# A decode-step kernel: second MLP layer on four column groups, folded output rows, early loads on two queues

## The chip, the cores and the metric

The kernel runs on one core of a Trainium2 chip. The metric is the device time of one execution in microseconds (us), lower is better. "Landing" is the moment at which a transfer's last bytes have arrived; "granted clock" is the share of TensorE's full clock that the profile shows in a stretch.

## The reference, cut to what matters

One decode step of a transformer block with modulation, for 8 batches: attention with grouped queries over a cache of 8192 positions, then an MLP with squared ReLU.

```python
mod = (_silu(c) @ w_mod).reshape(8, 6, 1, -1)          # sa, ca, ga, sb, cb, gb
h = _layernorm(x) * (1 + ca) + sa
x = x + ga * attention(h, k_cache, v_cache, wq, wo)     # caches: [8, 8, 8192, 128] bf16
h = _layernorm(x) * (1 + cb) + sb
r = relu(h @ w1 + b1); y = (r * r) @ w2 + b2            # w1: [512, 1792], w2: [1792, 512]
x = x + gb * y                                          # [8, 1, 512] bf16
```

The two caches are 268 MB; all other inputs together are about 15 MB.

## The kernel before

The caches come in 64 units of 4 MB (two heads of one batch each) into a ring of four slots. The MLP weights take over a slot at the very end, in six transfers. Every load but two of 8 KB (c and x) goes through SyncE's queue:

```python
# load n of the 64; d_w1/d_w2 come after the last of them
dep = [released.get(s), d_wo if n == NSLOT else None]
loaded[n] = dma("sync", s_ring[s], lambda e: e.dma_start(slot(s), src), dep)
...
load(0); load(1)            # ahead of A_wo in the queue
dma(... b1 ...); d_bb = dma(... b2 ...)
d_wo = dma("sync", s_wo, ...)
load(2); load(3)
...
d_w2 = [dma("sync", s_w2[i], ...) for i, (a, z, j) in
        enumerate(((0, 4, 4), (4, 8, 4), (8, 12, 4), (12, 14, 2)))]
```

The end of the program, with cuts. The activations are kept transposed (features on partitions), so the second layer uses the weights as the stationary operand and 8 batch columns as the moving one, and the result must be transposed back:

```python
for k in range(KT):                       # first layer: 4 x 14 matmuls, all f for each k
    if k == KT - 1: ...                   # variance, square root, reciprocal behind 42 of 56
    for f in range(FT): ...
for f in range(FT):                       # second layer
    for k in range(KT):
        matmul(yT_ps[:, k, :], W2v[:, f, k * 128:(k + 1) * 128], hidT[:, f, :],
               deps=[k_sq[f // 8], d_w2[f // 4]])
for cc in range(2): ...                   # residual x1T put into o_ps by 4 matmuls with IDENT
k_y2 = tensor_tensor(y2T, yT_ps, mod(5), mult)                 # 128x32
for cc in (1, 0):
    ... 2 matmuls: o_ps[64 * cc: 64 * cc + B] += y2T^T         # transposes back
    ... copy to out_sb: VectorE for one half, ScalarE for the other
    d_o.append(dma(("sync", "scalar")[cc], ...))               # 8 rows of 512 bytes each
Pg.wait("sync", d_o)
```

## Time and profile before

| | before |
|---|---|
| time, median of 3 | 668.38 us |
| span of the profiled execution | 666.7 us |
| bytes read | 283.66 MB |
| last landing of second-layer weights (landing records of the trace) | 663.33 us |
| output transfers issued | 664.85 and 664.92 us |
| last landing of the output | 666.27 us |

The page is read from its DMA rows: the transfers fill the span. The end is read from the timeline and from the landing records. The lines are shown in the prediction below.

### The profile page before, as it was taken

The page shows a single profiled execution, that of the slowest core. Times are in us where ns is not written, and L with a number is a line of the kernel's source. Part 1 is how long each engine was busy: PE and PEld are TensorE (multiplying, and loading weights), DVE is VectorE, ACT ScalarE, POOL GpSimd, SP SyncE. Part 2 cuts the span into 40 slices and gives each one's busy share as a digit, 9 for nine tenths or more (in the row PEclk, how much of TensorE's full clock was granted, in tenths as well). Part 3 has the DMA queues.
Part 4 walks back from the last instruction along what each step waited for, and adds up shares of the span by engine and source line. Part 5 has one row for each costly group of instructions (what it writes and reads, how often), then busy time and mean ns, then how long its engine had stood idle before and what let it go on. Part 6 is the DMA issues. An engine that isn't in the chain of part 4 may idle for free.

```text
span 666.7 us, 15924 instructions
## 1 busy us (share of the span) xinstructions
PE 528.3 (79%) x7259; PEld 352.2 (53%) x7259; DVE 307.9 (46%) x587; ACT 264.3 (40%) x307; POOL 20.5 (3%) x79
## 2 busy tenths in 40 slices
PE   3494976898849987599858988499776998589887
PEld 2383732675328742477316753287424773277535
DVE  1262741466316652367415662167513673146633
ACT  2151631466115651166314661166512663146611
POOL 7400000000000000000000000000000000000000
PEclk9696998799969999699998999799997999879996
DMA  9999999999999999999999999999999999999997
GB/s 375 437 406 441 419 433 433 425 434 431 438 427 433 433 434 427 434 434 425 434 431 438 427 431 434 434 427 431 438 425 434 433 436 427 431 434 434 427 420 285
DMA packets 12189, 283.85 MB, mean 426 GB/s; under 512 B 1261, under 2 KB 1297, under 8 KB 3601
## 3 DMA queue, kind: packets, MB, share of 16 engines
q1 hardware_dynamic: 12128, 283.65, 99.3%
q8 instruction: 9, 0.15, 0.1%
q10 hardware_dynamic: 48, 0.02, 0.0%
q14 instruction: 4, 0.02, 0.0%
HBM read 283.66 MB, written 0.01 MB: 425 GB/s over the span
## 4 chain that ended last, share of the span: by engine, by line
PE 52%; DMA 38%; ACT 6%; DVE 2%; issue 1%; SPq 0%; DVEq 0%
PE PS L488 36%; DMA ring<-in_A_k_cache_dram 33%; PE PS L505 9%; ACT P_sb L582 5%; DMA ring<-in_A_v_cache_dram 4%; DMA ring<-in_A_wq_dram 2%; PE PS L636 2%; PE PS L478 1%; ACT KTb L493 1%; DVE O_sb L656 1%; PE PS L472 1%; PE PS L594 1%; DVE Pm L608 0%; PE PS L614 0%; PE PS L773 0%
## 5 line engine op out<-in xcount | busy, mean ns | idle before, releaser
L488 PE MATMUL PS<-IDENT,ring 128*128 128x128 bf16 x4096 | 267.1, 227 | 56.2 <-DMA ring<-in_A_k_cache_dram 56.2
L488 PEld LDWEIGHTS PS<-IDENT,ring 128*128 128x128 bf16 x4096 | 246.5, 102 | 104.8 <-DMA ring<-in_A_k_cache_dram 57.4
L493 ACT ACTIVATE KTb<-PS 128x1024 bf16<-128x1024 bf16 x192 | 196.5, 1024 | 236.6 <-PE PS L488 236.6
L495 DVE COPY KTb<-PS 128x1024 bf16<-128x1024 bf16 x320 | 210.0, 688 | 146.5 <-PE PS L488 144.4
L636 PE MATMUL PS<-ring,Pm 128*32 128x512 bf16 x1018 | 67.2, 409 | 24.8 <-DMA ring<-in_A_v_cache_dram 23.9
L505 PE MATMUL PS<-KTb,Qb 128*32 128x512 bf16 x1024 | 79.0, 385 | 4.5 <-ACT KTb L493 4.5
L656 DVE CAST O_sb<-PS 128x512 bf16<-128x512 f32 x31 | 21.5, 692 | 112.7 <-PE PS L636 112.7
L636 PEld LDWEIGHTS PS<-ring,Pm 128*32 128x32 bf16 x1018 | 26.5, 101 | 61.8 <-DMA ring<-in_A_v_cache_dram 33.7
L535 ACT ACTIVATE KTb<-PS 32x192 bf16<-32x192 f32 (+1 forms) x18 | 5.6, 310 | 110.0 <-PE PS L472 103.9
L582 ACT ACTIVATE P_sb<-PS,negm 128x1024 bf16<-128x1024 f32 x32 | 35.2, 1111 | 20.2 <-DVE negm L577 20.2
L478 PE MATMUL PS<-ONES 128*128 128x512 f32 x80 | 42.1, 630 | 0.0
L472 PE MATMUL PS<-IDENT 128*128 128x512 bf16 x112 | 33.4, 380 | 0.0
L594 PE MATMUL PS<-IDENT,P_sb 128*128 128x128 bf16 x256 | 19.9, 220 | 15.4 <-ACT P_sb L582 15.4
L608 DVE COPY Pm<-PS 64x512 bf16<-64x512 bf16 x48 | 20.2, 421 | 25.0 <-PE PS L594 24.5
L594 PEld LDWEIGHTS PS<-IDENT,P_sb 128*128 128x128 bf16 x256 | 14.4, 98 | 25.1 <-ACT P_sb L582 25.1
L505 PEld LDWEIGHTS PS<-KTb,Qb 128*32 128x32 bf16 x1024 | 15.4, 94 | 21.0 <-ACT KTb L493 8.5
L512 DVE TENSOR_REDUCE m<-PS 128x1 f32<-128x512 f32 x32 | 22.1, 689 | 6.6 <-PE PS L505 6.6
L660 PEld LDWEIGHTS PS<-SEL,O_sb 128*128 128x128 bf16 x124 | 5.8, 97 | 30.0 <-DVE O_sb L656 30.0
L478 PEld LDWEIGHTS PS<-ONES 128*128 128x128 f32 x80 | 12.7, 190 | 10.6 <-issue 10.6
L660 PE MATMUL PS<-SEL,O_sb 128*128 128x8 bf16 x124 | 7.8, 169 | 12.3 <-DVE O_sb L656 12.0
L472 PEld LDWEIGHTS PS<-IDENT 128*128 128x128 bf16 x112 | 9.9, 104 | 10.1 <-issue 7.2
L543 PE MATMUL PS<-wo_sb,KTb 128*32 128x512 bf16 x192 | 11.8, 380 | 3.3 <-ACT KTb L535 3.3
(134 smaller groups left out, 147.0 us busy)
## 6 DMA issues: line engine op xcount, KB each, us to landing
ring<-in_A_k_cache_dram SPq DMA_DIRECT2D x32, 4096.0 KB, 34.0
ring<-in_A_v_cache_dram SPq DMA_DIRECT2D x31, 4096.0 KB, 27.8
ring<-in_A_wq_dram SPq DMA_DIRECT2D x1, 4096.0 KB, 19.8
wo_sb<-in_A_wo_dram SPq DMA_DIRECT2D x1, 4096.0 KB, 47.3
ring<-in_w_mod_dram SPq DMA_DIRECT2D x1, 3072.0 KB, 10.5
ring<-in_A_v_cache_dram SPq DMA_DIRECT2D x1, 2048.0 KB, 22.5
ring<-in_B_w_dram SPq DMA_DIRECT2D x3, 512.0 KB, 19.2
ring<-in_B_w_dram SPq DMA_DIRECT2D x1, 1344.0 KB, 17.8
```

The costliest lines, as they stand in the source:

```text
L472: ts = [op("tensor", lambda e: e.matmul(bank(at).rearrange("p (a r) -> p a r", a=4), IDENT[:, :], rhs)) for _ in range(n)]
L478: ts = [op("tensor", lambda e: e.matmul(bank(at).rearrange("p (a r) -> p a r", a=4), ONES[:, :], rhs)) for _ in range(n)]
L488: t = op("tensor", lambda e, j=j, i=i: e.matmul(STG[j][:, i, :], src[:, 32 * k + 8 * j + i, :], IDENT[:, :], is_transpose=True), [loaded[n ...
L493: stg_free[j] = op("scalar", lambda e, j=j, dst=dst: e.activation(dst, STG[j], ACT.Copy), [t])
L495: stg_free[j] = op("vector", lambda e, j=j, dst=dst: e.tensor_copy(dst, STG[j]), [t])
L505: t = op("tensor", lambda e, hf=hf, q=q, rhs=rhs: e.matmul(PS[32 * q:32 * (q + 1), k, :], Qb[:, 2 * p + hf, :], rhs, start=(p == 0 and hf ...
L512: return op("vector", lambda e: e.tensor_reduce(m4[:, k:k + 1], bank(k), AX.X, ALU.max), [t])
L582: exps.append(op("scalar", lambda e, k=k: e.activation(P_sb[:, k, :, :, :], bank(k).rearrange("p (i x) -> p i x", i=8).unsqueeze(2).to_bro ...
L594: t = op("tensor", lambda e, k=k, i=i: e.matmul(STG[k][:, i, :], P_sb[:, k, i, :, :].rearrange("p h x -> p (h x)"), IDENT[:, :], is_transp ...
L608: done.append(op("vector", lambda e, dst=dst, frm=frm: e.tensor_copy(dst, frm), [t, k_pm]))
L636: t = op("tensor", lambda e, m=m, cg=cg, p=p, vt=vt, Obank=Obank: e.matmul(Obank[32 * cg:32 * (cg + 1), :], lhs[:, p, 32 * m:32 * m + 32], ...
L656: t = op("vector", lambda e, osb=osb, Obank=Obank: e.tensor_copy(osb, Obank), [t])
```

## The change

Its intent has three parts. At the **end**, batches become the rows of the second layer's output: the hidden activations (128x32, 8 columns used) become the stationary operand, the weights move, and four blocks of 128 output columns go to four column groups of TensorE (32 columns of its array each, `tile_position=(0, 32 * k)`). The result is then already in output order, so the transposes back fall away; two additions fold four groups into two rows of 512 bytes. The first layer runs half by half. At the **start**, the first two loads and the biases go to ScalarE's queue and A_wo moves ahead of them; early copies go from ScalarE to VectorE; GpSimd builds fewer selection matrices. In the **loop**, four permute copies stay on VectorE and the projection goes behind 16 value matmuls.

```diff
-            dep = [released.get(s), d_wo if n == NSLOT else None]
+            dep = [released.get(s), d_wo if n == 2 * NSLOT - 1 else None, k_wm if eng == "scalar" else None]
...
-        k_mr1 = op("scalar", lambda e: e.activation(mod_r[:, 1, :], bank(1), ACT.Copy), [t])
+        k_mr1 = op("vector", lambda e: e.tensor_copy(mod_r[:, 1, :], bank(1)), [t])
...
-        load(0)
-        load(1)
-        dma("sync", s_bb, lambda e: e.dma_start(
+        load(0, "scalar")
+        load(1, "scalar")
+        dma("scalar", s_bb, lambda e: e.dma_start(
...
-        for k in range(KT):
-            if k == KT - 1:
+        for hh, (fa, fz) in enumerate(((0, 8), (8, FT))):
+            for k in range(KT):
+                if (hh, k) == (0, 2):
...
-                    yT_ps[:, k, :], W2v[:, f, k * 128:(k + 1) * 128], hidT[:, f, :],
-                    start=False, stop=(f == FT - 1), skip_group_check=True), [k_sq[f // 8], d_w2[f // 4]])
+                    y_ps[32 * k:32 * (k + 1), :], hidw[:, f, :], W2v[:, f, 128 * BLK[k]:128 * (BLK[k] + 1)],
+                    start=False, stop=(f == FT - 1), tile_position=(0, 32 * k), skip_group_check=True),
+                    [k_sq[f // 8], d_w2[f // 4]])
+        t = op("vector", lambda e: e.tensor_tensor(y_sb, y_ps, mod5[:], ALU.mult), [t])
+        for h in range(2):
+            rows = slice(64 * h, 64 * (h + 1))
+            t2 = op("vector", lambda e, h=h, rows=rows: e.tensor_tensor(
+                out_sb[:, h, :], y_sb[rows, :], x1_sb[rows, :], ALU.add), [t, k_res])
```

## The prediction

> **What bounds the kernel now.** I read the page first, its DMA rows and queue table before its engine rows. The engine rows say that TensorE is busy 79% of the span, which looks like a TensorE kernel; the DMA rows say otherwise. The columns of the DMA and GB/s rows are 40 equal slices of 16.7 us.
>
> ```profile
> DMA  9999999999999999999999999999999999999997
> GB/s 375 437 406 441 419 433 433 425 434 431 438 427 433 433 434 427 434 434 425 434 431 438 427 431 434 434 427 431 438 425 434 433 436 427 431 434 434 427 420 285
> ...
> q1 hardware_dynamic: 12128, 283.65, 99.3%
> ```
>
> The reader is to see that the transfers never pause: 283.65 MB go through one queue, 99.3% of all time of the 16 DMA engines is spent on its packets, and only the first and the last slice carry less. Divided by about 433 GB/s the bytes alone take some 655 us of a span of 666.7. The chain of waits agrees in its own way: DMA 38% of the span, and TensorE's 52% is mostly key tiles worked off between two loads that the chain also ends on. So everything between the first microseconds and the last load counts only through the DMA stream. The chance of a change lies in how early the stream starts, how evenly it runs, and what is left to do after its last byte.
>
> Then I read the windows at the end (start:end, length, busy time of PE, weight loads, VectorE, ScalarE, GpSimd, each with its count, then granted clock, DMA share, GB/s):
>
> ```profile
> 658.00:659.00 1.00, 0.72 (x22) 0.72 (x23) 0.51 (x3) 0.00 (x0) 0.00 (x0) 0.50 1.06 424
> 659.00:660.00 1.00, 1.00 (x27) 1.00 (x26) 0.00 (x0) 0.00 (x0) 0.00 (x0) 0.50 0.98 393
> 660.00:661.00 1.00, 0.68 (x16) 0.58 (x15) 0.32 (x2) 0.27 (x1) 0.00 (x0) 0.50 1.00 393
> 661.00:662.00 1.00, 0.32 (x12) 0.32 (x13) 0.88 (x5) 0.00 (x0) 0.00 (x0) 0.50 0.67 264
> 662.00:663.00 1.00, 0.87 (x34) 0.81 (x31) 0.21 (x1) 0.00 (x0) 0.00 (x0) 0.50 0.27 92
> 663.00:664.00 1.00, 1.00 (x27) 0.70 (x24) 0.19 (x1) 0.00 (x0) 0.00 (x0) 0.50 0.00 0
> ```
>
> The DMA share is full up to 661 us and gone by 663: the stream runs on underneath the whole MLP, because the MLP weights are its last 4 MB. The view of the tensor that holds these weights gives the last landing:
>
> ```profile
> L682 SPq DMA_DIRECT2D ring<-in_B_w_dram x4: 885/1444/5533, 641.0 to 649.9; - x4
> DMA to landing us min/median/max: 13.5/18.1/19.2
> ```
>
> The last of four pieces of the second layer's weights was issued at 649.9 and took 13.5 us to land: 663.4. (The landing records in the trace give 660.2, 661.5, 662.7 and 663.35 for the four pieces.) Now the timeline of the end:
>
> ```profile
> 661.68 2.06 PE L773 MATMUL PS<-KTb,ring 128*128 128x8 bf16 x56 [1.00 <-DVE KTb L768]
> ...
> 663.78 0.19 DVE L781 TENSOR_TENSOR KTb<-PS,modT 128x32 bf16<-128x32 f32 x1 [1.56 <-PE PS L773]
> ...
> 664.03 0.38 PE L786 MATMUL PS<-IDENT,KTb 128*8 128x128 bf16 x4
> 664.44 0.37 ACT L793 ACTIVATE KTb<-PS 8x256 bf16<-8x256 f32 x1 [3.90 <-PE PS L786]
> 664.49 0.41 DVE L791 CAST KTb<-PS 8x256 bf16<-8x256 f32 x1 [0.51 <-PE PS L786]
> 664.85 0.30 ACTq L794 DMA_DIRECT2D out_dram<-KTb  x1
> 664.92 0.31 SPq L794 DMA_DIRECT2D out_dram<-KTb  x1
> ```
>
> The reader is to see two limits that meet. The 56 second-layer matmuls run without a visible pause from 661.68 to 663.74, so the row names VectorE's square as what released them. But their last 8 need the piece that lands at 663.35, and by count they begin at 663.74 - 8 x 2.06/56 = 663.45. Had TensorE been ready any earlier, it would have waited for the weights.
>
> **What the Trainium skill says.** "DMA: Bandwidth & Descriptors", section "Where 436 GB/s comes from", gives a ceiling of 435.2 GB/s for a core's 16 engines; the steady slices above show 425 to 438, so the trace agrees: there is no rate left to win. The same page, "Issuing engines are not separate DMA queues", says that transfers issued from several engines run on the same 16 engines and interleave, and that only issue time is saved. The kernel before has no two large transfers on two queues at once, so its trace cannot show this; it is my reason to give the second queue no value. "TensorEngine Tiling (Array Packing)", section "Performance Considerations", proposes swapping stationary and moving operand with column tiling where one side is narrow, which is this change. The trace has the form already: 24 matmuls of L543 (128x32 stationary, 512 moving columns, four column groups) take 1.48 us, or 0.06 each. "VectorE: DVE Perf Modes", section "Two Vector instructions with no wait between them", says that an instruction whose operand starts in another group of 32 partitions than the last one's is held until earlier ones finish; nothing before shows it, but I count the two final adds as serial for it.
>
> **The change, part by part.**
>
> Start. Loads 0 and 1 move to ScalarE's queue and wait for the modulation matmul (about 14.8 us); the output-projection weights move ahead of them. The stream is full from about 2.5 us either way, and w_mod and A_wq, 7.3 MB, still cover it to about 21 us, so no gap opens. From 15 to some 42 us two queues share the engines. A_wq may land 2 to 3 us after the 21.1 us of now, and the first key tiles (30.8 now) start up to 4 us later. That delay is absorbed: the row for unit 2 shows TensorE idle 10.39 us for its load at 61.61, and the first value slot comes free at 96.0 with a load that takes 23.8 us to land although its own bytes need 9.7, so about 14 us of transfers lie queued ahead. Worth: 0.
>
> GpSimd loses some 40 selects (20.5 us busy now), ScalarE two copies of 0.6 us. GpSimd ends at 29.4, before the first keys at 30.8. Worth: 0. The permute copies in the loop go to VectorE, four of about 0.36 us instead of two, and the projection goes behind 16 value matmuls; in the loop they lie in the idle time of the V half. In the last batch: values from the landing at 649.4 to 650.45, projection 1.48 to 651.95, its copy 0.69 to 652.7; the next value matmuls wait for weights until 652.5 anyway, as now. Worth: 0.
>
> First layer. Now the variance matmul comes behind 42 of 56 matmuls; after, behind 16. From 658.28: 16 x 0.036 = 0.58, variance 0.57, so 659.4; square root, reciprocal and their gaps 0.6 as now, 660.0; the first half's matmuls end there too. Three VectorE steps of 0.25 give the first square at about 660.8 instead of 661.63: 0.8 us earlier. But this feeds the second layer, which now waits for the pieces at 660.2, 661.5, 662.7 and 663.35. The 0.8 us disappear.
>
> Second layer. 56 matmuls of 0.037 us (bound by 128-column weight loads) become 14 rounds of four, 128 moving columns each; at the granted clock of 0.50 a round is a quarter of the 0.43 us that L402's rounds of 512 columns took at that clock, 0.107 us: 1.5 us instead of 2.06. Only the last piece counts: two rounds, 0.21, and about 0.17 from start to result beyond the streaming (the 4 matmuls of L786 took 0.38 for two columns-passes of 0.107 per group). So 663.38 + 0.38 + 0.03 = 663.8. Now it is 663.74. Worth: 0.
>
> After the second layer. Out go the multiplication 0.19, four transposing matmuls 0.38, and the copies 0.37/0.41 with their gaps: 663.78 to 664.92. In come a multiplication of 128x128 and two additions of 64x128. VectorE's rows are 192 ns at 32 columns, 202 at 48, 222 to 225 at 64: about 160 + 1 per column, so 0.29 at 128. The additions, bf16 in SBUF, I take as 0.25. With gaps of 0.035: 663.82 + 0.29 + 0.035 + 0.25 + 0.035 + 0.25 = 664.68, transfers at 664.7 to 664.75. Saved: about 0.2 us. The output transfer (1.8 us to the end) has the same eight rows of 512 bytes on two queues.
>
> Sum: about -0.2 us of 668.38. I add another -0.1 because the slowest DMA engine, which sets each landing, trails the fastest by 2.2 us, and another mix of packets can only partly even that out. Predicted 668.1.
>
> **The rivals.** (1) The compute chain, not the weights, is the end's bound: then the 0.8 of the first layer, 0.5 of the second and 0.2 behind it all come through, 1.5 us, giving 666.9. For it: the timeline names VectorE as releaser, not the DMA. Against it: the landing at 663.35. (2) Two queues change the stream itself. The 4 KB rows of the output projection run at slices of 406 instead of 433; mixing them with 32 KB rows could hide up to 0.5 us of that, giving 667.6; or fetches of program code, which the trace shows stretching single packets from 1.2 to 1.7 us, fall on the slowest engine once more: 668.7. (3) The late A_wq starves the stream in the first batch. The queue would have to lose the 14 us; I see 4. It would make 670 or more.
>
> **Range and chances.** Bounded by rival 1 plus a little on one side and one bad code fetch on the other: 667.0 to 668.9. A gain of 2% would need 13 us, while start and tail together hold about 6; a loss of 2% needs rival 3 in earnest. So within 2%: 0.985.
>
> **What would show it.** The stream full from 2.5 us to about 661; the last weights landing at 663.0 to 663.7; TensorE waiting on the DMA for B_w2 pieces, where now no such wait appears; second-layer matmuls ending within 0.45 us of the last landing; about 0.9 us from there to the output transfers. I am wrong if the last landing moves by more than 0.5 us, if any slice before the last drops below 400 GB/s, or if the second layer ends well after the landing.

## The result, and the profile after

| | before | after |
|---|---|---|
| time, median of 4 in the same rounds | 668.42 us (668.37 to 669.41) | 668.65 us (668.50 to 668.85) |
| ratio, 95% interval | | 1.000 (0.9983 to 1.0017) |
| span of the profiled execution | 666.7 | 666.9 |
| A_wq landed / first key transposes | 21.0 / 30.83 | 23.2 / 31.82 |
| last landing of second-layer weights | 663.33 | 663.48 |
| last landing of the output | 666.27 | 666.25 |

A ratio is the mean time of one kernel's runs over that of the other's of the same rounds, so it is not quite the ratio of the medians. The numbers for landings are the last of the increments that the trace records for a transfer's semaphore, in us from the span's start.

The page of the changed kernel answers to the rows of before as follows (same columns):

```profile
GB/s 376 414 429 433 428 428 435 428 430 432 432 432 432 430 432 432 428 436 428 436 427 436 430 428 432 432 432 428 436 428 436 427 436 430 430 430 432 436 414 282
...
q1 hardware_dynamic: 11824, 275.26, 96.3%
q10 hardware_dynamic: 350, 8.41, 3.0%
```

The 8.4 MB of loads 0 and 1 and the biases are now on the second queue, and 96.3% + 3.0% of the engines' time is what one queue held before. The second and third slice, 437 and 406 before, are 414 and 429: the slower 4 KB rows of A_wo are spread over another time, and nothing is won in the sum. The start came as worked out; the first key tiles, before and then after:

```profile
30.84 5.71 PE L488 MATMUL PS<-IDENT,ring 128*128 128x128 bf16 x64 [5.11 <-DMA ring<-in_A_k_cache_dram]
```

```profile
31.82 6.43 PE L483 MATMUL PS<-IDENT,ring 128*128 128x128 bf16 x64 [3.81 <-DMA ring<-in_A_k_cache_dram]
```

They wait for load 0 in both, and start one microsecond later in the second. The windows of the changed kernel at the end:

```profile
661.00:662.00 1.00, 0.84 (x33) 0.70 (x32) 0.88 (x5) 0.00 (x0) 0.00 (x0) 0.50 0.62 246
662.00:663.00 1.00, 0.29 (x16) 0.06 (x8) 0.00 (x0) 0.00 (x0) 0.00 (x0) 0.50 0.33 119
663.00:664.00 1.00, 0.92 (x24) 0.47 (x24) 0.02 (x1) 0.00 (x0) 0.00 (x0) 0.50 0.00 0
```

Between 662 and 663 TensorE was busy 0.87 before and is busy 0.29 now: it stands idle, and the view of the weights' tensor says for what:

```profile
L676 SPq DMA_DIRECT2D ring<-in_B_w_dram x4: 432/2596/4702, 640.6 to 646.4; - x4
...
  PE PS L771: 0.7, 1
  PEld PS L771: 0.2, 1
...
DMA to landing us min/median/max: 17.0/18.6/20.0
```

The last piece, issued at 646.4, took 17.1 us to land by its landing record: 663.5. (The view's minimum of 17.0 is that of the piece before it.) No such wait for weights is named in the view of before. The last piece is issued 3.5 us earlier than before (646.4 against 649.9; why is not shown) and takes 3.6 us longer to land (17.1 against 13.5), so the earlier issue wins nothing. The timeline of the end:

```profile
661.19 1.07 PE L771 MATMUL PS<-ring,hidw 128*32 128x128 bf16 x32 [0.16 <-DVE hidw L766]
...
662.97 0.95 PE L771 MATMUL PS<-ring,hidw 128*32 128x128 bf16 x24 [0.71 <-DMA ring<-in_B_w_dram]
663.52 0.14 PEld L771 LDWEIGHTS PS<-ring,hidw 128*32 128x32 bf16 x8 [0.19 <-DMA ring<-in_B_w_dram]
663.98 0.29 DVE L775 TENSOR_TENSOR KTb<-PS,mod 128x128 bf16<-128x128 f32 x1 [2.03 <-PE PS L771]
664.30 0.45 DVE L778 TENSOR_TENSOR KTb<-KTb 64x128 bf16<-64x128 bf16 x2
664.78 0.37 SPq L781 DMA_DIRECT2D out_dram<-KTb  x1
664.78 0.31 ACTq L781 DMA_DIRECT2D out_dram<-KTb  x1
```

The second layer starts 0.49 us earlier than before (661.19 against 661.68), pauses twice for weights, and ends 0.2 us later (663.92 against 663.74), behind weights that landed 0.15 us later. Multiplication and two additions then take 0.8 us where multiplication, transposes and copies took 1.1.

### The profile page after: what moved, and what is told of

Its sections match the earlier page's. It is cut to its first block, busy times and chain, and to the rows that moved or that the text cites. A ratio compares the mean times of both kernels' runs of the same rounds, so it can differ in the third digit from the quotient of the medians.

```text
span 666.9 us, 15813 instructions
## 1 busy us (share of the span) xinstructions
PE 534.7 (80%) x7247; PEld 354.5 (53%) x7247; DVE 316.2 (47%) x611; ACT 257.6 (39%) x288; POOL 13.6 (2%) x37
## 3 DMA queue, kind: packets, MB, share of 16 engines
q1 hardware_dynamic: 11824, 275.26, 96.3%
## 4 chain that ended last, share of the span: by engine, by line
PE 53%; DMA 36%; ACT 7%; DVE 2%; SPq 1%; issue 1%; ACTq 0%; DVEq 0%
PE PS L483 36%; DMA ring<-in_A_k_cache_dram 33%; PE PS L500 9%; ACT P_sb L575 5%; DMA ring<-in_B_w_dram 3%; PE PS L629 2%; PE PS L473 1%; ACT KTb L488 1%; DMA KTb<-in_A_x_dram 1%; DVE O_sb L650 1%; SPq L676 1%; PE PS L467 1%; PE PS L587 1%; PE PS L393 1%; DVE Pm L601 1%
## 5 line engine op out<-in xcount | busy, mean ns | idle before, releaser
L629 PE MATMUL PS<-ring,Pm 128*32 128x512 bf16 x1018 | 69.8, 414 | 40.7 <-DMA ring<-in_A_v_cache_dram 39.8
L467 PE MATMUL PS<-IDENT 128*128 128x512 bf16 x104 | 31.7, 380 | 0.0
L654 PEld LDWEIGHTS PS<-R,O_sb 128*128 128x128 bf16 x124 | 5.7, 96 | 28.7 <-DVE O_sb L650 28.7
L536 PE MATMUL PS<-wo_sb,KTb 128*32 128x512 bf16 x192 | 18.9, 556 | 0.0
L654 PE MATMUL PS<-R,O_sb 128*128 128x8 bf16 x124 | 7.8, 169 | 12.4 <-DVE O_sb L650 12.0
L530 DVE CAST KTb<-PS 32x192 bf16<-32x192 f32 (+1 forms) x34 | 11.8, 346 | 6.1 <-PE PS L517 5.3
```

Source lines behind the costliest of these rows:

```text
L467: ts = [op("tensor", lambda e: e.matmul(bank(at).rearrange("p (a r) -> p a r", a=4), IDENT[:, :], rhs)) for _ in range(n)]
L629: t = op("tensor", lambda e, m=m, cg=cg, p=p, vt=vt, Obank=Obank: e.matmul(Obank[32 * cg:32 * (cg + 1), :], lhs[:, p, 32 * m:32 * m + 32], ...
```

## The experiments

My theory after the two traces: the DMA stream sets the end. What lies before it costs nothing, what lies beside it is hidden, and the three tenths of a microsecond behind it are the only thing that the change can move. The rivals were a cost of the second queue that hides a larger gain at the end, and a middle bound by TensorE. Twelve kernels ran (one of them is the changed kernel unedited, and one the padded kernel again), four to a call, each call on one chip and beside the kernel before.

### The two halves of the change alone

head_only is the changed kernel with the old end put back; tail_only is the kernel before with the new end. Together they hold each part of the change once.

```diff
 # head_only, from the changed kernel
-  (first layer by halves, y_ps on column groups, fold)
+  (old first layer, yT_ps, transposes back, two copies)
 # tail_only, from the kernel before: the reverse
```

> The changed kernel with the old second layer and output put back: early loads on two queues, early copies on VectorE, shorter GpSimd start, new order in the last-batch projection. Stream theory (the end is the last weight landing plus some 3.4 us): the stream is full either way, 668.4, within 0.2 of the kernel before. Rival, two queues cost the slowest DMA engine time: 668.6 to 668.9, and the last landing of the second-layer weights comes 0.2 to 0.4 us later than the 663.33 of before.

> The kernel before with only the new second layer, first-layer order and folded output. Stream theory: the 0.14 us by which the output transfers are issued earlier in the changed kernel, so 668.2 to 668.4. Rival, the two queues ate a larger gain of the tail: 667.9 or less.

Measured: head_only 668.88 us, tail_only 668.55, the kernel before 668.62 (ratios 1.0004 and 0.9996, intervals 0.9991 to 1.0017 and 0.9984 to 1.0008). The time of head_only fits the rival, but its stated sign is missing: its last weights landed at 663.23, no later than the 663.33 of before. So the 0.26 us, which lie within the interval, are made elsewhere. tail_only missed its 668.2 to 668.4; in its trace the last weights landed 0.3 us later than before, and that scatter is larger than the gain looked for. The landing records and SyncE's last instructions, read from the raw records of all traces, show where (us from the span's start; "branch" is SyncE's jump out of the program, which comes after its wait for the output):

```
kernel        weights  output   from weights  SyncE    from output
              landed   landed   to output     branch   to branch
before        663.33   666.27   2.94          666.34   0.07
head_only     663.23   666.18   2.95          666.61   0.43
before_half   659.27   662.22   2.95          662.30   0.08
after         663.48   666.25   2.77          666.49   0.24
tail_only     663.64   666.38   2.74          666.46   0.08
after_late    663.27   666.05   2.78          666.28   0.23
after_again   663.38   666.16   2.78          666.40   0.24
after_half    658.58   661.35   2.77          661.60   0.25
after_pad     663.43   666.21   2.78          666.23   0.02
after_pad2    662.96   665.72   2.76          665.74   0.02
after_nofold  663.29   666.15   2.86          666.17   0.02
```

Three things are to be read. The column "from weights to output" has two values: 2.94 to 2.95 with the old end, 2.74 to 2.78 with the new one. The new end is worth 0.16 to 0.21 us, about 0.17, whatever else differs. The column "from output to branch" has a gap of 0.23 to 0.43 in five kernels, all with the change's start, and 0.02 to 0.08 in the others. And the weights of the nine whole kernels of the table (all but the two cut by half) land between 662.96 and 663.64 without an order that follows the start: 663.33 and 663.64 with one queue, 662.96 to 663.48 with two. The 0.15 us by which they landed later in the changed kernel's first trace lie within this scatter. An effect of the second queue smaller than it, either way, is not excluded: only two of the nine traces have one queue.

### How much the computation has in reserve

Both kernels load only the first of four pieces of the second-layer weights and use it for all (wrong result). The landing then no longer holds the second layer up.

```diff
-  for i, (a, z, j) in enumerate(((0, 4, 4), (4, 8, 4), (8, 12, 4), (12, 14, 2)))]
+  for i, (a, z, j) in enumerate(((0, 4, 4),))]
...
-  W2v[:, f, ...],      [k_sq[f // 8], d_w2[f // 4]]
+  W2v[:, f % 4, ...],  [k_sq[f // 8], d_w2[0]]
```

> The kernel before, but only the first of four pieces of the second-layer weights is loaded and used for all (wrong result on purpose); 1.31 MB less at the end of the stream, some 3.1 us of it. If in the kernel before the chain of computation and the landings meet, as the prediction had it, taking the landings away gives almost nothing: 668.2 to 668.4. If the landing alone set its end, about 667.

> The same cut in the changed kernel (wrong result on purpose). Stream theory: its computation is ready about 1.2 us before the last landing, so without it the second layer ends at about 662.7 instead of 663.94 and the time is 667.4, 1.0 to 1.4 below the changed kernel and about 0.9 below the cut kernel before. If the new chain of computation is no shorter, there is no difference: 668.4.

Measured: 667.84 us for the cut kernel before (0.9983 of the whole one, 0.9969 to 0.9998), 667.15 for the cut changed kernel (0.9973, 0.9958 to 0.9987). The first is lower than the 668.2 to 668.4 of a tie; the second is lower than its 667.4 too, and the 0.69 us between them are less than the 0.9 expected. One row of each timeline tells why for the first: the second layer, first of the cut kernel before, then of the cut changed kernel.

```profile
661.47 1.65 PE L773 MATMUL PS<-KTb,ring 128*128 128x8 bf16 x56 [0.99 <-DVE KTb L768]
```

```profile
661.08 1.69 PE L771 MATMUL PS<-ring,hidw 128*32 128x128 bf16 x56 [0.17 <-DVE hidw L766]
```

The 56 old matmuls take 1.65 us when nothing holds them up, not the 2.06 of the whole kernel's row. That row had 0.41 us of pauses for weights merged into it. The trace of the kernel before shows one of them in the weight loads of the same matmuls, which come to a stop until 0.1 us after the third piece's landing at 662.69, with no releaser named:

```profile
662.80 0.86 PEld L773 LDWEIGHTS PS<-KTb,ring 128*128 128x128 bf16 x24 [0.19 <-issue]
```

The kernel before was bound by the landing, by about 0.4 us; I had read it as a tie. (The other 0.2 us between the traces of the whole and the cut kernel is an earlier start of the second layer, 661.47 against 661.68.) And the 56 new ones take 1.69: at the granted clock of 0.50 the swap of operands buys nothing on TensorE. What the change does win in the computation is the shorter first layer and the shorter way out. With the landings gone the times show 667.84 - 667.15 = 0.69 us of it, with the landings in place 0.17. The chain itself is shorter by more: from the first layer's first matmul to the last output issue it takes 664.30 - 658.07 = 6.23 us in the first trace and 663.62 - 658.50 = 5.12 in the second, 1.1 less. The first layer began 0.43 us later in the second trace, whose piece of weights landed 0.50 later; both lie within the scatter of the stream.

### Whether the stream really sets the end

The second half of one K load in batch 3 is left out in both kernels (wrong, though an average over 8192 nearly even weights hides it from the comparison).

```diff
+  w = UNIT // 2 if n == 24 else UNIT
-  loaded[n] = dma(eng, s_ring[s], lambda e: e.dma_start(slot(s), src), dep)
+  loaded[n] = dma(eng, s_ring[s], lambda e: e.dma_start(slot(s)[:, 0:w], src[:, 0:w]), dep)
```

> The changed kernel with the second half of one K load of batch 3 left out (wrong result on purpose): 2.10 MB less in the middle of the stream, at 431.7 GB/s 4.86 us. Stream theory: all of it comes through at the end, 663.6 to 664.0. Rival, TensorE's keys or the hand-over of slots bound the middle: less than half comes through, 666 or more.

> The same cut in the kernel before: stream theory 663.4 to 663.8; rival 666 or more.

Measured: 663.62 us for the changed kernel, whose uncut twin took 668.49: 4.87 less, and 4.86 was expected. The kernel before took 663.39 and 663.42 in two runs and 664.41 and 665.23 in two others (median 663.92, against 668.36); in its profiled run, one of the two longer ones, the last piece of weights landed 1.8 us behind the piece before it, where the traces in the table otherwise have 0.6 to 0.7. So I take the two lower runs, 4.94 and 4.97 less; by the medians it is 4.44. The edit takes bytes away and leaves TensorE's work as it was, and half a load in the middle comes through in full at the end: the middle is the stream, and TensorE's 80% is beside it.

One more trace is of a longer run: that of after_wmsplit below (677.11 us, its other runs 675.62 to 675.80), and its last piece is late by the same measure, 2.1 us behind the piece before it. The raw records say what held both up. A landing is the last of 16 increments of the transfer's semaphore, which I take as one from each DMA engine. In these two traces 15 of them had come by 658.08 and 670.73, and the last came at 659.27 and 672.18. The two packets of weights that are left by then start as a packet of 16 KB of program code (kind "instruction") ends: at 658.23, where the code takes 657.14 + 1.10 = 658.24, and at 671.13, where it takes 670.04 + 1.11 = 671.15. In the kernel before a fetch of the same size runs from 662.31 to 663.41, beside weight packets that go on every 0.08 us. By these times a fetch of code stood in front of the last weights on one DMA engine, and the 1.2 and 1.45 us that this cost are about what the two runs were longer by, 1.0 and 1.4. That the longer runs of the other sets have this cause is likely, but no trace of one was kept.

### How early the loads must start

Loads 0 and 1 wait for the use of A_wq instead of w_mod.

```diff
-  k_wm if eng == "scalar" else None
+  k_late if eng == "scalar" else None     # k_late: last matmul on A_wq
```

> The changed kernel, with loads 0 and 1 held back until A_wq has been used (about 27 us instead of 14.8). Stream theory: A_wo and load 2 keep the stream full, the first keys start 10 us or more later, and the queue of some 14 us ahead of TensorE absorbs it: 668.4 to 669.0. Rival, the stream starves in the first batch: 670 or more, and a slice below 400 GB/s between 80 and 130 us.

Measured: 668.52 us (ratio 1.0004, 0.9981 to 1.0021). Loads 0 and 1 were issued at 24.6 us; load 0 landed at 41.6 us instead of 31.8 and load 1 at 61.2 instead of 43.7, and the end did not move. Ten microseconds of delay in the first batch disappear in the queue of transfers, as the prediction had it.

### A first load in four parts

The 16 DMA engines finish w_mod 1.0 us apart (landing records of the changed kernel), and a transfer has landed when the last of them is done. I tried to have them start closer together.

```diff
-  d_wm = dma("sync", s_wm, lambda e: e.dma_start(RING[:, 2, 0:KT * NMOD], ...))
+  for i in range(4):
+      d_wm = dma("sync", s_wm, lambda e, i=i: e.dma_start(RING[32 * i:32 * (i + 1), 2, 0:KT * NMOD], ...))
```

> The changed kernel with the first load cut into four by partitions, so that the descriptors of all 16 DMA engines are made sooner. If the spread of 1.0 us between the first and the last engine at the landing of w_mod comes from descriptors made one after the other, it falls to 0.3 to 0.5 us, the last weights land up to 0.5 us earlier, and the time is 668.0 to 668.4. If the spread is made later, in the loads after it, or by the engines themselves, the last landing stays within 0.2 us of 663.5 and the time at 668.6.

Measured: 675.76 us, 1% slower (1.0103, 1.0089 to 1.0118). Neither expectation was near. The windows show the stretch from 6 to 8 us, first of this kernel, then of the changed one:

```profile
6.00:8.00 2.00, 0.00 (x0) 0.00 (x0) 0.00 (x0) 0.00 (x0) 2.00 (x2) 1.00 0.99 200
```

```profile
6.00:8.00 2.00, 0.00 (x0) 0.00 (x0) 0.00 (x0) 0.00 (x0) 2.00 (x2) 1.00 1.04 445
```

The engines' mean busy share is full in both (0.99 and 1.04), but they move 200 GB/s instead of 445: a packet of 24576 bytes takes 1913 ns (median) instead of 912. The Trainium skill, "SBUF — State Buffer", section "Door 1: The DMA port swizzle", says that bandwidth depends on how many of the 16 ports the partitions reach, and lists eight ports for partitions 0 to 31; half the ports, about half the rate, and the trace agrees. (No run separates the ports from other effects of the cut.) So the try says nothing on the spread of the engines. It says a lot on the stream: w_mod landed 18.6 - 11.1 = 7.5 us later than in the changed kernel, and the time is 675.76 - 668.61 = 7.15 us above the kernel before. What is lost at the start, too, comes through at the end.

### Without the fold

One addition over 128 partitions, four output transfers with rows of 256 bytes.

```diff
-  for h in range(2):
-      t2 = tensor_tensor(out_sb[:, h, :], y_sb[rows, :], x1_sb[rows, :], add)      # 64x128, twice
+  t2 = tensor_tensor(out_sb, y_sb, x1_sb, add)                                     # 128x128
+  d_o = [dma(("sync", "scalar")[k % 2], ..., outf[:, 128 * BLK[k]: ...], out_sb[32 * k:32 * k + B]) for k in range(4)]
```

> The changed kernel without the fold: one addition over 128 partitions in place of two over 64, and four output transfers of 256-byte rows in place of two of 512. Theory of short chains: one addition less, the first transfers issued 0.2 us earlier; but each queue issues two, 0.3 us apart, so the last issue is 0.1 us later: 668.5 to 668.8. Rival, rows under 512 bytes are slow to write: 669 or more.

Measured: 668.49 us (ratio 0.9995, 0.9983 to 1.0008; before 668.61). Its timeline:

```profile
663.79 0.29 DVE L775 TENSOR_TENSOR KTb<-PS,mod 128x128 bf16<-128x128 f32 x1 [2.26 <-PE PS L771]
664.12 0.23 DVE L776 TENSOR_TENSOR KTb<-KTb 128x128 bf16<-128x128 bf16 x1
664.37 0.72 SPq L778 DMA_DIRECT2D out_dram<-KTb  x2
664.38 0.65 ACTq L778 DMA_DIRECT2D out_dram<-KTb  x2
```

The first transfers go out 0.22 us sooner after the multiplication, and the second of each queue 0.3 to 0.4 us after the first. From the weights' landing to the output's it is 2.86 us against 2.77: the fold is worth 0.09 us in this one trace, half of what the whole new end wins. The times can't show it, since this kernel lacks the gap of the next section. Rows of 256 bytes did not show the cost that the rival gave them.

### The gap at SyncE's branch

> The changed kernel with five more SyncE instructions (waits that are long satisfied), in place of the five transfers that it issues less. In the two traces with the short SyncE program the last branch came 0.41 us after SyncE's last but one wait, in the traces with the long one 0.06 us. If the place of that branch in SyncE's program makes the gap, it falls to 0.06 us and the time to about 668.3 to 668.5, 0.2 to 0.3 below the changed kernel. If the gap comes from something else, it stays at 0.41 and the time at 668.6 to 668.8.

```diff
         load(3)
+        for d in (d_c, d_x, d_wm, d_wq, d_bb):
+            Pg.wait("sync", [d])
```

Measured: 668.38 us (ratio 0.9997, 0.9986 to 1.0009; before 668.61), and in the table above the gap is 0.02 us. The five waits appear as three more instructions in SyncE's trace, 85 instead of 82. One of them, for the biases, isn't long satisfied but ends at 43.2 us; the load behind it is issued at 43.4, as in the changed kernel (43.5). Over all traces the gap follows this number: all five with 82 instructions have it, and none of the others, with 79 (after_w2x, 0.02 us), 83 (after_nofold), 84, 85 or 87. With 82 the branch comes 0.41 us after SyncE's last wait instruction whenever the output lands, so the landing hides a part of it; head_only, whose output had landed before that wait, shows it whole. So the gap hangs on where the branch lies in SyncE's program, and the change, by moving five transfers off that queue, moved it to a bad place. What happens in the gap is not shown: no fetch of program code is recorded in it.

> The changed kernel once more, unedited, beside the padded one on one chip: 668.5 to 668.8, with the gap of some 0.2 us between the last landing of the output and SyncE's branch.

> The padded kernel once more, as the candidate that beats both: without the gap it should be 0.2 to 0.3 us below the changed kernel of the same call, and 0.1 to 0.3 below the kernel before; if the gap was a chance of two traces, no difference.

Measured: 668.49 us and 668.17, the kernel before 668.36; ratios to it 0.9995 (0.9982 to 1.0007) and 1.0001 (0.9987 to 1.0015, two runs near 669.7 among its six). The medians of the padded kernel are 0.2 us below the kernel before and 0.3 below the changed one, of which 0.22 is the gap; the rest is small against the scatter of the last landing (662.96 against 663.38 in the two traces). It is the best version that I found, but not by a margin that the intervals confirm.

## Why the prediction was right or wrong

The range of 667.0 to 668.9 around the predicted 668.1 held 668.65, and "within 2%" was right; none of the three signs of being wrong came: the last landing moved by 0.15 us, the second layer was done 0.45 us after it, and no slice between the first and the last fell under 414 GB/s (the first, 376, was 375 before too). That is a hit of the mechanism, the stream, and not of the small sum: the forecast -0.3 us came out as +0.1 to +0.2 by medians that scatter as much, and a range six times as wide as the effect would have held either. By its own steps:

- **The stream bounds the kernel.** Right, and shown from both sides: 2.10 MB less gave 4.87 us less, a start 7.5 us late gave 7.15 us more.
- **Start, worth 0.** Right. A_wq landed 2.2 us later (2 to 3 predicted), the first keys started 1.0 us later (up to 4), and a delay of ten microseconds more still cost nothing. The second queue showed no value and no cost in the landings beyond their scatter.
- **Loop and GpSimd, worth 0.** They ran together with the start, in head_only and in the changed kernel, never alone. The projection of the last batch ended at 651.9, as worked out. Not foreseen: TensorE's clock fell to half at 655.3 instead of 656.2, so that the last partial sums took 1.00 us instead of 0.59 and the first layer began at 658.62 instead of 658.28. The reserve before the landing absorbed it. In the other whole kernels of the table the clock fell between 655.9 and 658.1, with both starts, so nothing ties this to the change.
- **First layer, 0.8 us earlier and hidden.** Right in size: from its first matmul to the second layer's first it took 2.57 us instead of 3.40. Hidden by the landing, as said; with the landings gone it is part of the 1.1 us by which the chain is shorter.
- **Second layer, "1.5 us instead of 2.06".** Both terms were mis-sized. 2.06 held 0.41 us of pauses that the timeline had merged into one row; the matmuls are 0.029 us each, not 0.037, and the new ones 0.030 (1.69 / 14 = 0.121 a round of four, where scaling down a round of 512 columns gave 0.107). With it falls "two limits that meet": the landing alone bound the kernel before. The worth of 0 stood because of the landing, not by this sum. Last landing to last result was 0.45 us, as predicted.
- **After the second layer, -0.2.** The sum came out right, -0.17, with luck in it. The output transfers are issued 0.29 us sooner after the landing (1.30 us against 1.59 for the last one), more than forecast; but from there to the output's landing it takes 1.43 to 1.47 us in the folded kernels with the new end and 1.34 to 1.35 with the old one. The prediction took this as equal; why it is not stays open. Its two additions ran one after the other (0.45 us in a row, one takes 0.22, where two rows on the same partitions overlap: 660.91 + 0.23 and 661.06), as it had read in "VectorE: DVE Perf Modes", section "Two Vector instructions with no wait between them".
- **-0.1 for a better balance of the engines.** Nothing of it was seen; the last landing scatters by 0.7 us between kernels with the same bytes.
- **What the sum left out.** SyncE's last branch: 0.24 us after the output's landing instead of 0.07, which takes back the 0.17. In the two first traces that leaves the landing that is 0.15 us later, which is scatter, and the measured difference is 0.1 to 0.2 us on the other side of zero instead of -0.3.

Rival 1, a gain of 1.5 us through a bound by computation, fell with the wait for weights in the trace after; even with the landings taken away the times gained 0.69. Rival 3, that the stream starves, fell with after_late. Rival 2, that two queues change the stream by -0.8 to +0.3 us, found no support in the landings, but its smaller sizes are no larger than the 0.7 us by which they scatter. Its other half, a fetch of program code on the slowest engine, is what the two traces of longer runs show, with both starts; in the changed kernel's trace the fetch (662.48 to 663.58) did not hold up the last weights, so that its 668.7 is near the measured 668.65 is chance.

## What to carry to other kernels

Where the transfers fill the span, look for the last landing and count only what lies behind it: here 3 us of 668, of which a rewritten end could win 0.17. A timeline row that merges many instructions can hide pauses, so test a tie between computation and landing by taking the landing away. And when the expected gain is a few tenths, read it as the distance between two events in many traces, not from medians.

## What the Trainium skill lacked or had wrong

- "TensorEngine Tiling (Array Packing)", "Performance Considerations": it proposes the swap with column tiling for a narrow side; of limits it names an overhead per matmul, which doesn't tell that nothing is won here. 56 matmuls took 1.65 us before and 1.69 us after the swap, at a granted clock of 0.50.
- "DMA: Bandwidth & Descriptors", "Issuing engines are not separate DMA queues": it gives no size for what interleaving costs a single transfer. A_wq landed at 23.2 instead of 21.0 us with the second queue beside it, while the last weights landed at 662.96 to 663.48 with two queues, 663.33 and 663.64 with one.
- The gap at the end of SyncE's program: "Runtime: NRT & Kernel Launch", "Instruction fetch mechanics", has a stall for fetching the target of a taken branch, without a size. Here the gap lies before the branch and no fetch is recorded in it: 0.23 to 0.43 us between the last landing of the output and the branch in five kernels, 0.02 us in the same program with five waits more.
- No page that I read has a size for what a fetch of program code does to a transfer on the same DMA engine: 16 KB of code took 1.1 us, and in two traces the last weights landed 1.2 and 1.45 us after the 15 increments before.
- No page that I read has how much the last landing of one and the same amount of bytes scatters: 0.7 us over the nine whole kernels.
